# Attention backward pass: dK and dV through column tiles in bursts of four units, crossbar transfers of 1 MB for 512 KB, and TensorE in emission order

## The chip, the cores and the metric

The kernel runs on one core of one Trainium2 chip. The metric is the device time of one execution in microseconds (us), lower is better. Engines: TensorE (PE; its weight loads are PEld), VectorE (DVE), ScalarE (ACT), GpSimd (POOL), and SyncE (SP), whose queue issues the crossbar transfers.

## The reference, cut to what matters

The reference is one transformer block (softmax attention with 32 heads of width 16, sequence 2048, then a squared-ReLU layer) and its gradients for all inputs. Only the attention gradients matter here. For one head, with P the softmax numerators and O the attention output:

```python
scores = einsum('bhqd,bhkd->bhqk', q, k) * scale
p = softmax(scores)
o = einsum('bhqk,bhkd->bhqd', p, v)
# gradients, as the kernel forms them (softmax division and row sums are
# already folded into the operands stored by earlier phases):
#   dS = P * dP          dP = dO V^T
#   dV = P^T dO          dK = dS^T Q          dQ = dS K
```

## The kernel before

The attention backward pass works on *units*: 128 queries, 512 keys, two heads. There are 1024 of them: 8 head groups x 2 head pairs x 4 key chunks x 16 query blocks. dK and dV contract over the queries, which lie on the partitions, so dS and P can be used as they are. dQ contracts over the keys, so dS must be transposed first; a DMA through the crossbar does this. The loop before, cut:

```python
LAG, LAGQ = 2, 3
pup = tile_pool("p5pu", bufs=5); dsp = tile_pool("p5ds", bufs=5); dtp = tile_pool("p5dt", bufs=5)
stp = tile_pool("p5st", bufs=2, space=PSUM); dpp = tile_pool("p5dp", bufs=2, space=PSUM)
...
def kv(u):        # dK, dV of one unit: dS and P are the weights, Q and dO (16 columns) move
    for a in range(2):
        for sub in range(4):
            matmul(acc[:, 0, a, sub, :], lhsT=ds[:, a, sub * P:(sub + 1) * P], rhs=T["Q"][:, ib, col:col + DH], ...)
            matmul(acc[:, 1, a, sub, :], lhsT=pu[:, a, sub * P:(sub + 1) * P], rhs=T["dO"][:, ib, col:col + DH], ...)
    ...
def dq(u):        # dQ of two units: transposed dS is the weights, K (16 columns) moves
    for i in range(2):
        for a in range(2):
            for sub in range(4):
                matmul(accq[:, ib0 + i, a, :], lhsT=dsT[:, (i * 2 + a) * 4 + sub, :], rhs=T["K"][...], ...)
...
for ib0 in range(0, ST, 2):                      # two units
    ds2 = dsp.tile([P, 2, 2, 512], BF16)
    for i in range(2):
        ...                                      # two 512-column matmuls to st, two to dp
        for a in range(2):
            scalar.activation(pu[:, a, :], sts[a][:], Exp, scale=self.scale)
        if len(pend) >= LAG:
            kv(pend.pop(0))
        vector.tensor_tensor(ds2[:, i], dp[:], pu[:], mult)
        pend.append(...)
    dsT = dtp.tile([P, 16, P], BF16)
    sync.dma_start_transpose(dsT[:], ds2[...])   # 512 KB through the crossbar
    if len(pendq) >= LAGQ:
        dq(pendq.pop(0))                         # dQ three transfers behind
    pendq.append(...)
```

The framework's scheduler orders the instructions of each engine.

The softmax here doesn't subtract the row's maximum and nothing guards it: scores larger than these inputs give would overflow.

Of the kernel before, what the change touches and what calls it, by code (L numbers as in the profile page):

```python
# [8 lines left out]
BF16 = mybir.dt.bfloat16  # L9
F32 = mybir.dt.float32  # L10
ACT = mybir.ActivationFunctionType
ALU = mybir.AluOpType
# [6 lines left out]
P = 128  # L19
DH = 16  # L20
# [13 lines left out]
class K:  # L34
# [219 lines left out]
    def phase12(self):  # L254
# [8 lines left out]
        with tc.tile_pool(name="p12", bufs=1) as sb, tc.tile_pool(name="p12e", bufs=8) as eb:  # L263
# [116 lines left out]
            with tc.tile_pool(name="p2c", bufs=1) as cp, tc.tile_pool(name="p2q", bufs=2) as qp, \  # L380
# [12 lines left out]
                for pidx in range(2 * NQ):  # L393
                    g, jp = divmod(pidx, 2)
                    heads = [4 * g + 2 * jp + a for a in range(2)]
                    if jp == 0:
                        T = self.load_quad(qp, srcs, g)
                    KT = T["KT"]
                    self.load_masked(masked, {"QT": (self.QTq_d, 0)}, g, jp)
# [47 lines left out]
                out[n].append(t)  # L447
        return out

    def load_masked(self, masked, srcs, g, jp):  # L450
        nc = self.nc
        for n, (src, sh) in srcs.items():
            for a in range(2):
                j = 2 * jp + a
                r = 32 * ((j + sh) % 4)
                for (c0, cw) in chunks(self.S, 512):
                    nc.sync.dma_start(masked[n][j][r:r + 32, c0:c0 + cw], src[g, r:r + 32, c0:c0 + cw])

    def load_quad(self, pool, srcs, g):
        nc = self.nc  # L460
# [613 lines left out]
    def attn_bwd(self):  # L1074





        tc, nc = self.tc, self.nc  # L1080
        S, D, H, NQ, ST, SC = self.S, self.D, self.H, self.NQ, self.ST, self.SC
        LAG, LAGQ = 2, 3
        W = 4 * DH
        with ExitStack() as es:
            qp = es.enter_context(tc.tile_pool(name="p5q", bufs=2))
            pup = es.enter_context(tc.tile_pool(name="p5pu", bufs=LAG + 3))
            dsp = es.enter_context(tc.tile_pool(name="p5ds", bufs=5))
            dtp = es.enter_context(tc.tile_pool(name="p5dt", bufs=LAGQ + 2))
            stp = es.enter_context(tc.tile_pool(name="p5st", bufs=2, space=PSUM))
            dpp = es.enter_context(tc.tile_pool(name="p5dp", bufs=2, space=PSUM))  # L1090
            accp = es.enter_context(tc.tile_pool(name="p5acc", bufs=1, space=PSUM))
            acckv = accp.tile([P, 2, 2, 2, 4, DH], F32, name="acckv")
            accq = accp.tile([P, ST, 2, DH], F32, name="accq")
            tm = {"K": self.ktm_d, "Q": self.qtm_d, "dO": self.dOp_d}
            fm = {"QT": self.QTq_d, "dOT": self.dOTq_d}
            cp = es.enter_context(tc.tile_pool(name="p5c", bufs=1))
            masked = self.make_masked(cp, ["KT", "VT"])
            pend, pendq = [], []

            def load_group(g):  # L1100
                T = {}
                for n, src in fm.items():
                    t = qp.tile([P, S], BF16, name=f"{n}q")
                    nc.gpsimd.dma_start(t[:], src[g])  # L1104
                    T[n] = t
                for n, src in tm.items():
                    t = qp.tile([P, ST, W], BF16, name=f"{n}g")
                    with nc.allow_non_contiguous_dma(reason="128B runs"):
                        nc.gpsimd.dma_start(t[:], src.rearrange("(st p) d -> p st d", p=P)[:, :, g * W:(g + 1) * W])
                    T[n] = t  # L1110
                return T

            def kv(u):
                (T, g, jp, c, ib, acc, pu, ds) = u
                if ib == 0:
                    nc.vector.memset(acc, 0.0)
                for a in range(2):
                    col = (2 * jp + a) * DH
                    for sub in range(4):
                        nc.tensor.matmul(acc[:, 0, a, sub, :], lhsT=ds[:, a, sub * P:(sub + 1) * P],  # L1120
                                         rhs=T["Q"][:, ib, col:col + DH], start=False, stop=False, skip_group_check=True)
                        nc.tensor.matmul(acc[:, 1, a, sub, :], lhsT=pu[:, a, sub * P:(sub + 1) * P],  # L1122
                                         rhs=T["dO"][:, ib, col:col + DH], start=False, stop=False, skip_group_check=True)
                if ib == ST - 1:
                    h0 = 4 * g + 2 * jp
                    d = self.dk_t[:, 4 * c:4 * c + 4, h0 * DH:(h0 + 2) * DH].rearrange("p s (a d) -> p a s d", a=2)
                    nc.vector.tensor_scalar(d, acc[:, 0], self.scale, None, ALU.mult)
                    d = self.dv_t[:, 4 * c:4 * c + 4, h0 * DH:(h0 + 2) * DH].rearrange("p s (a d) -> p a s d", a=2)
                    nc.vector.tensor_copy(d, acc[:, 1])

            def dq(u):
                (T, g, jp, c, ib0, dsT) = u
                if c == 0 and ib0 == 0:
                    nc.vector.memset(accq[:], 0.0)
                for i in range(2):
                    for a in range(2):
                        col = (2 * jp + a) * DH
                        for sub in range(4):
                            nc.tensor.matmul(accq[:, ib0 + i, a, :], lhsT=dsT[:, (i * 2 + a) * 4 + sub, :],  # L1139
                                             rhs=T["K"][:, 4 * c + sub, col:col + DH], start=False, stop=False,  # L1140
                                             skip_group_check=True)
                if c == SC - 1 and ib0 == ST - 2:
                    h0 = 4 * g + 2 * jp
                    d = self.dq_t[:, :, h0 * DH:(h0 + 2) * DH].rearrange("p s (a d) -> p s a d", a=2)
                    nc.vector.tensor_scalar(d, accq[:], self.scale, None, ALU.mult)

            T = load_group(0)
            n = 0
            for g in range(NQ):
                Tn = load_group(g + 1) if g + 1 < NQ else None  # L1150
                for jp in range(2):
                    self.load_masked(masked, {"KT": (self.KTq_d, 0), "VT": (self.VTq_d, 2)}, g, jp)
                    for c in range(SC):
                        c0 = 512 * c
                        acc = acckv[:, n % 2]
                        n += 1
                        for ib0 in range(0, ST, 2):
                            ds2 = dsp.tile([P, 2, 2, 512], BF16, name="ds")
                            for i in range(2):
                                ib = ib0 + i  # L1160
                                q = slice(ib * P, (ib + 1) * P)
                                sts = [stp.tile([P, 512], F32, name="st") for a in range(2)]
                                dp = dpp.tile([P, 2, 512], F32, name="dp")
                                for a in range(2):
                                    nc.tensor.matmul(sts[a][:], lhsT=T["QT"][:, q], rhs=masked["KT"][2 * jp + a][:, c0:c0 + 512],  # L1165
                                                     start=True, stop=True)
                                for a in range(2):
                                    nc.tensor.matmul(dp[:, a, :], lhsT=T["dOT"][:, q], rhs=masked["VT"][2 * jp + a][:, c0:c0 + 512],  # L1168
                                                     start=True, stop=True)
                                pu = pup.tile([P, 2, 512], BF16, name="pu")  # L1170
                                for a in range(2):
                                    nc.scalar.activation(pu[:, a, :], sts[a][:], ACT.Exp, scale=self.scale)  # L1172
                                if len(pend) >= LAG:
                                    kv(pend.pop(0))
                                nc.vector.tensor_tensor(ds2[:, i], dp[:], pu[:], ALU.mult)  # L1175
                                pend.append((T, g, jp, c, ib, acc, pu, ds2[:, i]))
                            dsT = dtp.tile([P, 16, P], BF16, name="dsT")
                            nc.sync.dma_start_transpose(dsT[:], ds2[:].rearrange("p i a k -> p (i a k)"))
                            if len(pendq) >= LAGQ:
                                dq(pendq.pop(0))  # L1180
                            pendq.append((T, g, jp, c, ib0, dsT))
                T = Tn
            while pend:
                kv(pend.pop(0))
            while pendq:
                dq(pendq.pop(0))

    def phase6(self):
        tc, nc, pp, io = self.tc, self.nc, self.pp, self.io
# [261 lines left out]
```

## Time and profile before

The kernel before takes 3542 us (median of 4 runs, 3530 to 3552). The attention backward pass fills 1646 to 3342 us of the profiled run, 1696 us, about half the span.

The first fence has lines of the profile page's groups of instructions. Columns: line, engine, operation, output and inputs with shapes, count; then busy us and mean ns of one; then the idle time of that engine just before them and what ended most of it.

```profile
L1172 ACT ACTIVATE pu<-st 128x512 bf16<-128x512 f32 x2048 | 1114.5, 594 | 573.7 <-PE st L1165 572.3
L1175 DVE TENSOR_TENSOR ds<-dp,pu 128x1024 bf16<-128x1024 f32 x1024 | 1245.8, 1222 | 391.1 <-ACT pu L1172 251.2
L1165 PE MATMUL st<-KTm,QTq 128*128 128x512 bf16 x2048 | 655.2, 384 | 8.0 <-issue 6.8
L1120 PE MATMUL acckv<-Qg,ds 128*128 128x16 bf16 x8192 | 532.1, 170 | 25.8 <-issue 2.9
L1139 PE MATMUL accq<-Kg,dsT 128*128 128x16 bf16 x8192 | 311.8, 170 | 125.2 <-DMA dsT<-ds 123.1
```

ScalarE waits mostly for TensorE's scores, VectorE for ScalarE, and TensorE seldom waits for anything except the transposed dS. TensorE bounds the pass, by this reading. The next fence, the view of busy time in a stretch, shows the whole pass: TensorE is busy 1543 of 1696 us, at 0.97 of its full clock.

```profile
core 0: us, PE busy (x) PEld busy (x) DVE busy (x) ACT busy (x) POOL busy (x), PEclk, DMA share, GB/s
1646.00:3342.00 1696.00, 1542.76 (x28167) 1016.88 (x28675) 1298.95 (x1251) 1117.68 (x2052) 32.79 (x36) 0.97 1.08 173
```

The timeline of an undisturbed stretch comes next. Columns: start and length in us, engine, line, operation, count, and in brackets the idle time before and what ended it.

```profile
3200.34 5.16 SPq L1178 DMA_TRANSPOSE dsT<-ds  x2
3200.36 0.66 PE L1165 MATMUL st<-KTm,QTq 128*128 128x512 bf16 x2
3200.63 2.49 DVE L1175 TENSOR_TENSOR ds<-dp,pu 128x1024 bf16<-128x1024 f32 x2 [0.32 <-ACT pu L1172]
3200.78 1.08 ACT L1172 ACTIVATE pu<-st 128x512 bf16<-128x512 f32 x2 [0.18 <-PE st L1165]
...
3201.70 0.55 PE L1139 MATMUL accq<-Kg,dsT 128*128 128x16 bf16 x16
3202.10 0.59 PE L1165 MATMUL st<-KTm,QTq 128*128 128x512 bf16 x2
3203.36 0.66 PE L1165 MATMUL st<-KTm,QTq 128*128 128x512 bf16 x2
```

From the scores at 3200.36 to those at 3203.36, two units, pass 3.00 us: 1.50 us a unit. The sixteen dQ matmuls at 3201.70 follow without a wait. The waits view of 1700 to 3300 us (total us, times, longest) shows that such waits exist, but are not the rule:

```profile
ACT pu L1172 <- PE st L1165: 543.7, 929, 9.5
PEld L1139 <- DMA dsT<-ds: 155.9, 97, 9.0
PE accq L1139 <- DMA dsT<-ds: 117.1, 83, 8.1
```

The last two lines see the same stalls twice, once from the weight load and once from the matmul, so they must not be added. More than half of this, and every long one, lies at the start or near a change of the head group, while the next group's loads are in flight as well.

Taking the end of the last ds instruction, the transfer's landing (its last semaphore update) and the start of the first dQ weight load from the trace, a 512 KB transfer lands 6.2 us after ds is ready (median; nine in ten between 4.6 and 9.7), and dQ starts 7.55 us after ds (median). Landed data waits for TensorE for 1.0 us (median), but in 120 of 512 transfers it is TensorE that waits for the landing (dQ starts within 0.1 us of it).

### The profile page before, as it was taken

Reading aid. Unit: us, or ns where it says so; the run is one execution under the profiler, and the core shown is the slowest. Engines: PE = TensorE matmul, PEld = TensorE weight load, DVE = VectorE, ACT = ScalarE, POOL = GpSimd, SP = SyncE. Lnnn points to the kernel's source line nnn. Section 1 sums busy time; section 2 is a strip of 40 time slices with the busy share of each in tenths; the row PEclk is TensorE's granted clock in tenths of the full one; section 3 lists DMA queues with packets and bytes.
Section 4 is the critical chain, followed back from the end, with each engine's and each line's share of the span. In section 5 each row is a group of like instructions: output and inputs, shape, how many; then the busy total and the mean of one; then the engine's idle time right before and its main releaser. Section 6 shows DMA issues by size and latency. Waiting matters only on the chain. (4 is left out here: it accounts for less than half of the span.)

```text
span 3518.2 us, 99351 instructions
## 1 busy us (share of the span) xinstructions
PE 3006.1 (85%) x42822; PEld 1747.5 (50%) x43588; DVE 1908.0 (54%) x2886; ACT 2347.3 (67%) x3545; POOL 251.4 (7%) x343
## 2 busy tenths in 40 slices
PE   5999998888876878487997979989799998999977
PEld 2455543333333333265664656656566665666633
DVE  6222220000004366355886868878687786888855
ACT  3999999999982334333765756756566675767633
POOL 3111110000001014311000000000000000000000
PEclk7999999999997989699998989999899999999998
DMA  3111110000013355655999999999999999999952
GB/s 119 63 50 50 45 38 12 12 6 12 5 49 139 113 196 192 189 154 131 174 179 155 178 162 172 176 174 175 161 175 183 176 178 159 180 178 173 176 185 65
DMA packets 1190469, 449.43 MB, mean 128 GB/s; under 512 B 1097354, under 2 KB 1161484, under 8 KB 1190028
## 3 DMA queue, kind: packets, MB, share of 16 engines
q1 hardware_dynamic: 1159900, 361.61, 57.5%
q0 software_dynamic: 21504, 71.71, 6.9%
q10 hardware_dynamic: 8624, 9.70, 0.8%
q8 instruction: 341, 5.59, 0.6%
q14 instruction: 100, 0.82, 0.1%
HBM read 106.83 MB, written 67.64 MB: 50 GB/s over the span
## 5 line engine op out<-in xcount | busy, mean ns | idle before, releaser
L1172 ACT ACTIVATE pu<-st 128x512 bf16<-128x512 f32 x2048 | 1114.5, 594 | 573.7 <-PE st L1165 572.3
L1175 DVE TENSOR_TENSOR ds<-dp,pu 128x1024 bf16<-128x1024 f32 x1024 | 1245.8, 1222 | 391.1 <-ACT pu L1172 251.2
L412 ACT ACTIVATE pu<-st 128x1024 bf16<-128x1024 f32 x1024 | 940.1, 1376 | 4.7 <-PE accbank L418 4.7
L1165 PE MATMUL st<-KTm,QTq 128*128 128x512 bf16 x2048 | 655.2, 384 | 8.0 <-issue 6.8
L409 PE MATMUL st<-QTm,KTq 128*128 128x512 bf16 x1864 | 566.7, 377 | 6.9 <-ACT pu L412 1.5
L1120 PEld LDWEIGHTS <-ds 128*128 128x128 bf16 x8192 | 502.4, 96 | 119.0 <-issue 8.3
L1120 PE MATMUL acckv<-Qg,ds 128*128 128x16 bf16 x8192 | 532.1, 170 | 25.8 <-issue 2.9
L1122 PE MATMUL acckv<-dOg,pu 128*128 128x16 bf16 x8192 | 528.0, 169 | 0.0
L1122 PEld LDWEIGHTS <-pu 128*128 128x128 bf16 x8192 | 460.4, 96 | 118.3 <-issue 8.4
L418 PEld LDWEIGHTS <-pu 128*128 128x128 bf16 x8192 | 291.2, 96 | 458.7 <-ACT pu L412 408.2
L1168 PE MATMUL dp<-VTm,dOTq 128*128 128x512 bf16 x1539 | 508.7, 385 | 0.5 <-DMA dOTq<-dOTq_d 0.5
L418 PE MATMUL accbank<-Vaug,pu 128*128 128x17 bf16 x8192 | 353.5, 172 | 93.4 <-ACT pu L412 38.1
L1139 PE MATMUL accq<-Kg,dsT 128*128 128x16 bf16 x8192 | 311.8, 170 | 125.2 <-DMA dsT<-ds 123.1
L1139 PEld LDWEIGHTS <-dsT 128*128 128x128 bf16 x8192 | 263.5, 96 | 192.4 <-DMA dsT<-ds 164.6
L1168 PEld LDWEIGHTS <-dOTq 128*128 128x128 bf16 x2048 | 188.4, 97 | 244.7 <-issue 81.3
L427 DVE RECIPROCAL rl<-accbank 128x4 f32<-128x4 f32 x128 | 23.0, 180 | 526.0 <-PE accbank L418 525.6
L288 DVE TENSOR_SCALAR ev_fm<-pps,bcol 128x512 bf16<-128x512 f32 x92 | 69.1, 751 | 195.4 <-PE pps L281 185.7
L409 PEld LDWEIGHTS <-KTq 128*128 128x128 bf16 x2048 | 129.7, 96 | 35.4 <-issue 20.5
L1165 PEld LDWEIGHTS <-QTq 128*128 128x128 bf16 x2048 | 128.9, 96 | 11.1 <-issue 8.1
L281 PE MATMUL pps<-xhat1T,wpad 128*128 128x512 bf16 x372 | 119.9, 378 | 7.8 <-DVE ev_fm L288 3.8
L1104 POOL DMA_DIRECT2D QTq<-QTq_d x8 | 4.5, 558 | 1184.0 <-PE dp L1168 1156.4
L544 ACT ACTIVATE rT<-ups,bias 128x512 bf16<-128x512 f32 x56 | 38.5, 687 | 52.1 <-PE ups L542 52.0
(298 smaller groups left out, 2260.2 us busy)
## 6 DMA issues: line engine op xcount, KB each, us to landing
dsT<-ds SPq DMA_TRANSPOSE x512
rT_d<-rT SPq DMA_DIRECT2D x4, 1792.0 KB
rT<-rT_d SPq DMA_DIRECT2D x4, 1792.0 KB
duT_d<-duT POOLq DMA_DIRECT2D x4, 1792.0 KB, 12.0
rT_f<-rT_d SPq DMA_DIRECT2D x14, 512.0 KB
duT_f<-duT_d POOLq DMA_DIRECT2D x14, 512.0 KB, 4.1
xhat_d<-xhat SPq DMA_DIRECT2D x2, 2048.0 KB
QTq_d<-ev_fm POOLq DMA_DIRECT2D x32, 128.0 KB, 2.1
```

The source lines that it names most:

```text
L281: nc.tensor.matmul(pt[:, :sw], lhsT=wpads[t][:, kt, g, :], rhs=xhat1T[:, kt, s0:s0 + sw], start=(kt == 0), stop=(kt == DT - 1))
L288: nc.vector.tensor_scalar(ev[:, :sw], pt[:, :sw], bc, None, ALU.add)
L409: nc.tensor.matmul(stt[:, a, :qw], lhsT=KT[:, kb * P:(kb + 1) * P], rhs=QTm[a][:, q0:q0 + qw], start=True, stop=True)
L412: nc.scalar.activation(pu[:, :, :qw], stt[:, :, :qw], ACT.Exp, scale=self.scale)
L418: nc.tensor.matmul(acc[:, a, sub, :], lhsT=pu[:, a, sub * P:(sub + 1) * P], rhs=Vaug[:, kb, heads[a], :], start=False, stop=False, skip_gr ...
L1120: nc.tensor.matmul(acc[:, 0, a, sub, :], lhsT=ds[:, a, sub * P:(sub + 1) * P], rhs=T["Q"][:, ib, col:col + DH], start=False, stop=False, s ...
L1122: nc.tensor.matmul(acc[:, 1, a, sub, :], lhsT=pu[:, a, sub * P:(sub + 1) * P], rhs=T["dO"][:, ib, col:col + DH], start=False, stop=False, ...
L1139: nc.tensor.matmul(accq[:, ib0 + i, a, :], lhsT=dsT[:, (i * 2 + a) * 4 + sub, :], rhs=T["K"][:, 4 * c + sub, col:col + DH], start=False, s ...
L1165: nc.tensor.matmul(sts[a][:], lhsT=T["QT"][:, q], rhs=masked["KT"][2 * jp + a][:, c0:c0 + 512], start=True, stop=True)
L1168: nc.tensor.matmul(dp[:, a, :], lhsT=T["dOT"][:, q], rhs=masked["VT"][2 * jp + a][:, c0:c0 + 512], start=True, stop=True)
L1172: nc.scalar.activation(pu[:, a, :], sts[a][:], ACT.Exp, scale=self.scale)
L1175: nc.vector.tensor_tensor(ds2[:, i], dp[:], pu[:], ALU.mult)
```

## The change

The intent is to shorten TensorE's work. With dS and P as the *moving* operand, dK and dV need four 512-column matmuls per unit in place of sixteen pairs of weight load and 16-column matmul. Each of the four has 16 weight columns and occupies one of four column tiles of the array, so that they can run side by side. Because a change of tiling was expected to have a price, the matmuls of four units are done in one burst. The result is now transposed, so 16 TensorE transposes per head pair turn it back ("turn"). The crossbar transfers hold four units (1 MB), TensorE runs in emission order, and the masked K and V loads move to GpSimd's queue, one head pair earlier. The diff, condensed to its core; the turn, the copies of the results, the masked loads and the tail are cut:

```diff
-        LAG, LAGQ = 2, 3
+        G = 4
-            pup bufs=5, dsp bufs=5, dtp bufs=5          (tiles of two units)
+            pup bufs=9, dsp bufs=3, dtp bufs=3          (ds and dsT: four units)
-            acckv = accp.tile([P, 2, 2, 2, 4, DH], F32, name="acckv")
+            acckv = accp.tile([P, 512], F32, name="acckv")
 def kv(u):
+                for j, (n, src) in enumerate((("Q", ds), ("dO", pu))):
+                    for a in range(2):
+                        r = 64 * j + 32 * a
+                        nc.tensor.matmul(acckv[r:r + DH, :], lhsT=T[n][:, ib, col:col + DH], rhs=src[:, a, :],
+                                         start=(ib == 0), stop=(ib == ST - 1))
+            with tc.manual_schedule(engines={mybir.EngineType.PE}):
+                            for ib0 in range(0, ST, G):
+                                dsg = dsp.tile([P, G, 2, 512], BF16, name="ds")
+                                for i in range(G):
+                                    ...                       # scores, [turn], dP, exponentials, product
+                                    pend.append(...)
+                                    if len(pendq) > G:
+                                        dq(pendq.pop(0))      # one unit of dQ
+                                    if i == 1 and len(pend) >= G + 2:
+                                        r = kv_group()        # the burst: four units of kv
+                                dsT = dtp.tile([P, 8 * G, P], BF16, name="dsT")
+                                nc.sync.dma_start_transpose(dsT[:], dsg[:].rearrange("p i a k -> p (i a k)"))
+                                for i in range(G):
+                                    pendq.append((T, g, jp, c, ib0 + i, i, dsT))
```

How far dQ trails the scores is set by the test `len(pendq) > G`: the queue holds eight units when a group begins, so dQ of a unit is emitted eight units after its scores.

More of the change, by code (lines that the diff above doesn't have):

```diff
@@ L448, in make_masked, with load_masked @@
         return out
-    def load_masked(self, masked, srcs, g, jp):
+    def load_masked(self, masked, srcs, g, jp, eng=None):
         nc = self.nc
+        eng = eng or nc.sync
         for n, (src, sh) in srcs.items():
@@ L456, in load_masked @@
                 for (c0, cw) in chunks(self.S, 512):
-                    nc.sync.dma_start(masked[n][j][r:r + 32, c0:c0 + cw], src[g, r:r + 32, c0:c0 + cw])
+                    eng.dma_start(masked[n][j][r:r + 32, c0:c0 + cw], src[g, r:r + 32, c0:c0 + cw])
     def load_quad(self, pool, srcs, g):
@@ L1085, in attn_bwd @@
             qp = es.enter_context(tc.tile_pool(name="p5q", bufs=2))
-            pup = es.enter_context(tc.tile_pool(name="p5pu", bufs=LAG + 3))
-            dsp = es.enter_context(tc.tile_pool(name="p5ds", bufs=5))
-            dtp = es.enter_context(tc.tile_pool(name="p5dt", bufs=LAGQ + 2))
+            pup = es.enter_context(tc.tile_pool(name="p5pu", bufs=9))
+            dsp = es.enter_context(tc.tile_pool(name="p5ds", bufs=3))
+            dtp = es.enter_context(tc.tile_pool(name="p5dt", bufs=3))
+            kvp = es.enter_context(tc.tile_pool(name="p5kv", bufs=2))
             stp = es.enter_context(tc.tile_pool(name="p5st", bufs=2, space=PSUM))
@@ L1091, in attn_bwd @@
             accp = es.enter_context(tc.tile_pool(name="p5acc", bufs=1, space=PSUM))
-            acckv = accp.tile([P, 2, 2, 2, 4, DH], F32, name="acckv")
+            acckv = accp.tile([P, 512], F32, name="acckv")
+            nc.vector.memset(acckv[:], 0.0)
             accq = accp.tile([P, ST, 2, DH], F32, name="accq")
@@ L1096, in attn_bwd @@
             cp = es.enter_context(tc.tile_pool(name="p5c", bufs=1))
+            kvs = cp.tile([P, 1], F32, name="kvs")
+            nc.vector.memset(kvs[0:64], self.scale)
+            nc.vector.memset(kvs[64:P], 1.0)
             masked = self.make_masked(cp, ["KT", "VT"])
@@ L1113, in kv, with turn, dq @@
             def kv(u):
-                (T, g, jp, c, ib, acc, pu, ds) = u
-                if ib == 0:
-                    nc.vector.memset(acc, 0.0)
+                (T, g, jp, c, ib, kvT, pu, ds) = u
+                for j, (n, src) in enumerate((("Q", ds), ("dO", pu))):
+                    for a in range(2):
+                        r = 64 * j + 32 * a
+                        col = (2 * jp + a) * DH
+                        nc.tensor.matmul(acckv[r:r + DH, :], lhsT=T[n][:, ib, col:col + DH], rhs=src[:, a, :],
+                                         start=(ib == 0), stop=(ib == ST - 1))
+                if ib == ST - 1:
+                    nc.vector.tensor_scalar(kvT[:, 512 * c:512 * (c + 1)], acckv[:], kvs[:], None, ALU.mult)
+            def turn(g, jp, kvT):
+                h0 = 4 * g + 2 * jp
+                tp = dpp.tile([P, ST, P], BF16, name="dp")
+                for st in range(ST):
+                    nc.tensor.transpose(tp[:, st, :], kvT[:, st * P:(st + 1) * P], self.ident[:])
+                v = tp[:].rearrange("p s (t a e) -> p t s a e", t=2, a=2)
+                for t, dst in enumerate((self.dk_t, self.dv_t)):
+                    d = dst[:, :, h0 * DH:(h0 + 2) * DH].rearrange("p s (a d) -> p s a d", a=2)
+                    nc.scalar.copy(d, v[:, t, :, :, 0:DH])
+            def dq(u):
+                (T, g, jp, c, ib, i, dsT) = u
+                if c == 0 and ib == 0:
+                    nc.vector.memset(accq[:], 0.0)
                 for a in range(2):
@@ L1119, in kv @@
                     for sub in range(4):
-                        nc.tensor.matmul(acc[:, 0, a, sub, :], lhsT=ds[:, a, sub * P:(sub + 1) * P],
-                                         rhs=T["Q"][:, ib, col:col + DH], start=False, stop=False, skip_group_check=True)
-                        nc.tensor.matmul(acc[:, 1, a, sub, :], lhsT=pu[:, a, sub * P:(sub + 1) * P],
-                                         rhs=T["dO"][:, ib, col:col + DH], start=False, stop=False, skip_group_check=True)
-                if ib == ST - 1:
-                    h0 = 4 * g + 2 * jp
-                    d = self.dk_t[:, 4 * c:4 * c + 4, h0 * DH:(h0 + 2) * DH].rearrange("p s (a d) -> p a s d", a=2)
-                    nc.vector.tensor_scalar(d, acc[:, 0], self.scale, None, ALU.mult)
-                    d = self.dv_t[:, 4 * c:4 * c + 4, h0 * DH:(h0 + 2) * DH].rearrange("p s (a d) -> p a s d", a=2)
-                    nc.vector.tensor_copy(d, acc[:, 1])
-            def dq(u):
-                (T, g, jp, c, ib0, dsT) = u
-                if c == 0 and ib0 == 0:
-                    nc.vector.memset(accq[:], 0.0)
-                for i in range(2):
-                    for a in range(2):
-                        col = (2 * jp + a) * DH
-                        for sub in range(4):
-                            nc.tensor.matmul(accq[:, ib0 + i, a, :], lhsT=dsT[:, (i * 2 + a) * 4 + sub, :],
-                                             rhs=T["K"][:, 4 * c + sub, col:col + DH], start=False, stop=False,
-                                             skip_group_check=True)
-                if c == SC - 1 and ib0 == ST - 2:
+                        nc.tensor.matmul(accq[:, ib, a, :], lhsT=dsT[:, (i * 2 + a) * 4 + sub, :],
+                                         rhs=T["K"][:, 4 * c + sub, col:col + DH], start=False, stop=False,
+                                         skip_group_check=True)
+                if c == SC - 1 and ib == ST - 1:
                     h0 = 4 * g + 2 * jp
@@ L1145, in dq @@
                     nc.vector.tensor_scalar(d, accq[:], self.scale, None, ALU.mult)
-            T = load_group(0)
-            n = 0
-            for g in range(NQ):
-                Tn = load_group(g + 1) if g + 1 < NQ else None
-                for jp in range(2):
-                    self.load_masked(masked, {"KT": (self.KTq_d, 0), "VT": (self.VTq_d, 2)}, g, jp)
-                    for c in range(SC):
-                        c0 = 512 * c
-                        acc = acckv[:, n % 2]
-                        n += 1
-                        for ib0 in range(0, ST, 2):
-                            ds2 = dsp.tile([P, 2, 2, 512], BF16, name="ds")
-                            for i in range(2):
-                                ib = ib0 + i
-                                q = slice(ib * P, (ib + 1) * P)
-                                sts = [stp.tile([P, 512], F32, name="st") for a in range(2)]
-                                dp = dpp.tile([P, 2, 512], F32, name="dp")
-                                for a in range(2):
-                                    nc.tensor.matmul(sts[a][:], lhsT=T["QT"][:, q], rhs=masked["KT"][2 * jp + a][:, c0:c0 + 512],
-                                                     start=True, stop=True)
-                                for a in range(2):
-                                    nc.tensor.matmul(dp[:, a, :], lhsT=T["dOT"][:, q], rhs=masked["VT"][2 * jp + a][:, c0:c0 + 512],
-                                                     start=True, stop=True)
-                                pu = pup.tile([P, 2, 512], BF16, name="pu")
-                                for a in range(2):
-                                    nc.scalar.activation(pu[:, a, :], sts[a][:], ACT.Exp, scale=self.scale)
-                                if len(pend) >= LAG:
-                                    kv(pend.pop(0))
-                                nc.vector.tensor_tensor(ds2[:, i], dp[:], pu[:], ALU.mult)
-                                pend.append((T, g, jp, c, ib, acc, pu, ds2[:, i]))
-                            dsT = dtp.tile([P, 16, P], BF16, name="dsT")
-                            nc.sync.dma_start_transpose(dsT[:], ds2[:].rearrange("p i a k -> p (i a k)"))
-                            if len(pendq) >= LAGQ:
-                                dq(pendq.pop(0))
-                            pendq.append((T, g, jp, c, ib0, dsT))
-                T = Tn
@@ L1183, in attn_bwd, with kv_group @@
-            while pend:
-                kv(pend.pop(0))
-            while pendq:
-                dq(pendq.pop(0))
+            def kv_group():
+                for u in pend[:G]:
+                    kv(u)
+                (T, g, jp, c, ib, kvT, pu, ds) = pend[G - 1]
+                del pend[:G]
+                return (g, jp, kvT) if c == SC - 1 and ib == ST - 1 else None
+            msrc = {"KT": (self.KTq_d, 0), "VT": (self.VTq_d, 2)}
+            self.load_masked(masked, msrc, 0, 0)
+            T = load_group(0)
@@ new lines, in attn_bwd @@
+            turnq = []
+            with tc.manual_schedule(engines={mybir.EngineType.PE}):
+                for g in range(NQ):
+                    Tn = load_group(g + 1) if g + 1 < NQ else None
+                    for jp in range(2):
+                        if 2 * g + jp + 1 < 2 * NQ:
+                            self.load_masked(masked, msrc, (2 * g + jp + 1) // 2, 1 - jp, eng=nc.gpsimd)
+                        kvT = kvp.tile([P, S], BF16, name="kvT")
+                        for c in range(SC):
+                            c0 = 512 * c
+                            for ib0 in range(0, ST, G):
+                                dsg = dsp.tile([P, G, 2, 512], BF16, name="ds")
+                                for i in range(G):
+                                    ib = ib0 + i
+                                    q = slice(ib * P, (ib + 1) * P)
+                                    sts = [stp.tile([P, 512], F32, name="st") for a in range(2)]
+                                    for a in range(2):
+                                        nc.tensor.matmul(sts[a][:], lhsT=T["QT"][:, q], rhs=masked["KT"][2 * jp + a][:, c0:c0 + 512],
+                                                         start=True, stop=True)
+                                    if turnq and i == 3:
+                                        turn(*turnq.pop(0))
+                                    dp = dpp.tile([P, 2, 512], F32, name="dp")
+                                    for a in range(2):
+                                        nc.tensor.matmul(dp[:, a, :], lhsT=T["dOT"][:, q], rhs=masked["VT"][2 * jp + a][:, c0:c0 + 512],
+                                                         start=True, stop=True)
+                                    pu = pup.tile([P, 2, 512], BF16, name="pu")
+                                    for a in range(2):
+                                        nc.scalar.activation(pu[:, a, :], sts[a][:], ACT.Exp, scale=self.scale)
+                                    nc.vector.tensor_tensor(dsg[:, i], dp[:], pu[:], ALU.mult)
+                                    pend.append((T, g, jp, c, ib, kvT, pu, dsg[:, i]))
+                                    if len(pendq) > G:
+                                        dq(pendq.pop(0))
+                                    if i == 1 and len(pend) >= G + 2:
+                                        r = kv_group()
+                                        if r:
+                                            turnq.append(r)
+                                dsT = dtp.tile([P, 8 * G, P], BF16, name="dsT")
+                                nc.sync.dma_start_transpose(dsT[:], dsg[:].rearrange("p i a k -> p (i a k)"))
+                                for i in range(G):
+                                    pendq.append((T, g, jp, c, ib0 + i, i, dsT))
+                    T = Tn
+                turn(*kv_group())
+                while pendq:
+                    dq(pendq.pop(0))
```

## The prediction

It was made from the kernel, the diff and the profile before alone.

> **What bounds it now.** The attention backward pass runs from about 1646 to 3342 us (timeline): 1024 units of four 512-column matmuls, two exponentials, one product, 16 dK/dV ("kv") and 8 dQ weight-load/matmul pairs. In undisturbed stretches (timeline, 3200 to 3235 us) a unit takes 1.50 us, TensorE at full granted clock: wide matmuls 0.85 us, kv 0.41, dQ 0.27. ScalarE needs 1.09 us a unit, VectorE 1.25. 1024 x 1.50 is 1536 us; the other 160 us are mostly seven stalls of about 20 us at the head-group changes (windows near 1860, 2080, 2510 us), where the group's loads compete with the crossbar transfers.
>
> The crossbar is nearly as tight. From the trace's DMA packets and semaphore updates: one 512 KB transfer per 3.0 us; three quarters are issued only after the previous issue ended, then about every 2.9 us. Alone, one lands about 5 us after ds is ready: 1.1 us to the first packet, about 2.45 of packets, over 1 to landing. Undisturbed, dQ starts 7.5 us after ds is ready (timeline), so there are 2.5 us of slack.
>
> **What changes.** kv goes from 0.41 to about 0.21 to 0.28 us a unit: four 512-column matmuls in four column tiles, if they overlap, as the Trainium skill says in TensorEngine Tiling (Array Packing), section Key Properties; it also says that changing the mode drains TensorE, hence the bursts. No run here shows either yet. TensorE's need falls to about 1.35 to 1.40 us a unit; VectorE, about 1.29, is next. About a third of the stage's TensorE instructions go, so fewer instruction fetches interrupt the transfers; masked loads leave SyncE's queue.
>
> **Where it is lost.** A transfer now holds four units: it starts only when the fourth is done and takes about 2.45 us longer, about 7.3 us to landing (estimate: 5 + 2.45). dQ of group n-2 begins in the first unit of group n, on an in-order TensorE: at 1.40 us a unit that leaves only 5 x 1.40 + 0.85 - 2.75 = 5.1 us. The loop over two groups is landing 7.3 + dQ 0.27 + wide 0.85 + dQ 0.27 + burst 1.1 + wide 0.85 + dQ 0.27 + last unit's scores to ds ready 2.75 (timeline) = 13.7 us for eight units: 1.7 us a unit instead of 1.50. Before, this loop has room. With faster packets (1.85 us per 512 KB, seen for short times) it would be 1.55. So TensorE's gain turns into waiting for dsT. At 1.62 to 1.70 us a unit plus about 100 us for group changes and the start the stage takes 1760 to 1840 us.
>
> **Prediction.** 3630 us, 3430 to 3750 us 8 times in 10. Faster by over 2%: 0.22; within 2%: 0.28; slower by over 2%: 0.50.
>
> **What would show it.** Right: the waits view shows TensorE waiting for dsT far above the present 117 us, mostly before the first dQ of each group of four; 1 MB transfers landing 6.5 to 8 us after ds is ready; kv bursts near 1 us. Wrong on tiles: bursts of 3 us or more (no overlap; well slower). Wrong on the loop: dsT waits stay small and units take 1.4 us.
>
> **What would make it wrong.** The larger transfers may stream without the gaps now seen between small ones, or at the fast packet rate with fewer instruction fetches; then VectorE or TensorE bounds the unit at 1.35 to 1.45 us and the kernel gains 3 to 5%. Group-change stalls may shrink with the masked loads a pair earlier.

## The result, and the profile after

The changed kernel takes 3825 us (median of 4 runs, 3815 to 3836), and its results are correct. Ratios here are the mean time of one kernel's fast runs over that of the other's of the same rounds, so not quite the ratio of the quoted medians: 1.080, 95% interval 1.075 to 1.085. The kernel became slower by 8%. The prediction said slower, but by 2.5%, and its range ended at 3750.

The pass now takes 1641 to 3639 us, 1998 us for 1696; nothing else in the program became longer. The groups of instructions after:

```profile
L1194 ACT ACTIVATE pu<-st 128x512 bf16<-128x512 f32 x2048 | 1105.6, 594 | 859.5 <-PE st L1184 857.9
L1184 PE MATMUL st<-KTm,QTq 128*128 128x512 bf16 x2048 | 700.1, 400 | 39.8 <-DMA dOTq<-dOTq_d 7.4
L1149 PE MATMUL accq<-Kg,dsT 128*128 128x16 bf16 x8192 | 362.3, 171 | 366.8 <-DMA dsT<-ds 326.6
L1127 PE MATMUL acckv<-ds,Qg 128*16 128x512 bf16 x2048 | 321.5, 444 | 0.6 <-DVE ds L1195 0.6
```

The idle time before the dQ matmuls went from 125 to 367 us, and ScalarE's wait for scores from 572 to 858 us. The waits of 1700 to 3600 us (the stretch is longer, because the pass is):

```profile
ACT pu L1194 <- PE st L1184: 825.8, 665, 15.0
PEld L1149 <- DMA dsT<-ds: 399.1, 156, 15.0
PE accq L1149 <- DMA dsT<-ds: 310.0, 130, 14.5
```

And the pass as one stretch. The clock that the throttle granted fell from 0.97 to 0.91:

```profile
1641.00:3639.00 1998.00, 1596.32 (x16643) 728.85 (x16642) 1289.77 (x1128) 1124.66 (x2084) 145.72 (x263) 0.91 0.82 147
```

A piece of the timeline shows both what the change gained and where it was lost:

```profile
3400.44 10.91 SPq L1204 DMA_TRANSPOSE dsT<-ds  x2
...
3401.12 0.35 PE L1149 MATMUL accq<-Kg,dsT 128*128 128x16 bf16 x8
3401.40 0.39 PE L1127 MATMUL acckv<-ds,Qg 128*16 128x512 bf16 x2
3401.41 0.39 PE L1127 MATMUL acckv<-pu,dOg 128*16 128x512 bf16 x2
3401.62 0.38 PE L1127 MATMUL acckv<-ds,Qg 128*16 128x512 bf16 x2
...
3402.37 0.60 PE L1184 MATMUL st<-KTm,QTq 128*128 128x512 bf16 x2
...
3404.58 0.35 PE L1149 MATMUL accq<-Kg,dsT 128*128 128x16 bf16 x8
...
3405.21 0.59 PE L1190 MATMUL dp<-VTm,dOTq 128*128 128x512 bf16 x2
...
3408.22 0.36 PE L1149 MATMUL accq<-Kg,dsT 128*128 128x16 bf16 x8 [2.42 <-DMA dsT<-ds]
```

The gain: the first four burst matmuls start within 0.01 us (3401.40 and 3401.41, two each), the next four 0.21 us later. Four matmuls on four column tiles take the time of one, and the burst from 3401.40 to the next scores at 3402.37 takes 0.97 us for four units.

The loss: the transfer issued at 3400.44 is needed by the dQ at 3408.22, 7.78 us later. TensorE was ready for it after the dP matmuls of 3405.21 and stood still for 2.42 us. As TensorE works in order, the scores behind that dQ wait too, and with them ScalarE, VectorE, and the next transfer.

This is a closed loop over two groups of four units: the ds of group n is ready, its transfer lands, its dQ starts while the units of group n + 2 are computed, the ds of group n + 2 is ready, its transfer starts. The terms, read from the trace for every group, with what the prediction had put in. The last column leaves out the 38 of 254 loops that touch a change of the head group, because the prediction counted those changes apart:

```
                                         predicted   measured, mean (median)   away from changes, mean
ds ready -> transfer landed                 7.3        7.7 (7.1) us                 7.3
landed -> first dQ                          0          0.8 (0.04)                   0.8
first dQ -> ds of group n + 2 ready         6.4        7.0 (6.6)                    6.9
sum: two groups, eight units               13.7       15.5                         15.0
```

The mean before rounding is 15.53 us; 128 times that is 1988 us, for a pass of 1998. Before, the same eight units took 4 x 3.30 = 13.2 us on average, stalls included. The short two-group periods of the changed kernel (one in twenty) are 13.0 us (6.73 to dQ, 6.23 after it): the same loop with nothing in its way.

The 0.8 us between landing and dQ can be followed in the trace. In 170 of 256 groups dQ starts within 0.3 us of the landing. The other 86 hold 196 of the 204 us in sum. In all 86 TensorE had stood still before the dQ of the group just before (for 2.8 us, median), in 81 of them until that group's own landing, and after the next landing it was still busy with the work in between, for all but 7 of the 196 us. So the loops of the even and of the odd groups delay each other on the one TensorE that works in order.

### The profile page after: what moved, and what is told of

Read it like the earlier page. It is cut to its first block, busy times and chain, and to the rows that moved or that the text cites. A ratio compares the mean times of both kernels' runs of the same rounds, so it can differ in the third digit from the quotient of the medians.

```text
span 3814.2 us, 75626 instructions
## 1 busy us (share of the span) xinstructions
PE 3094.9 (81%) x31556; PEld 1460.3 (38%) x31556; DVE 1894.1 (50%) x2761; ACT 2354.2 (62%) x3577; POOL 371.1 (10%) x583
## 5 line engine op out<-in xcount | busy, mean ns | idle before, releaser
L1184 PE MATMUL st<-KTm,QTq 128*128 128x512 bf16 x2048 | 700.1, 400 | 39.8 <-DMA dOTq<-dOTq_d 7.4
L1149 PE MATMUL accq<-Kg,dsT 128*128 128x16 bf16 x8192 | 362.3, 171 | 366.8 <-DMA dsT<-ds 326.6
L1190 PE MATMUL dp<-VTm,dOTq 128*128 128x512 bf16 x2048 | 648.4, 400 | 0.3
L1149 PEld LDWEIGHTS <-dsT 128*128 128x128 bf16 x8192 | 351.0, 98 | 676.1 <-DMA dsT<-ds 419.9
L418 PEld LDWEIGHTS <-pu 128*128 128x128 bf16 x8192 | 291.2, 96 | 458.7 <-ACT pu L412 408.2
L1127 PE MATMUL acckv<-ds,Qg 128*16 128x512 bf16 x2048 | 321.5, 444 | 0.6 <-DVE ds L1195 0.6
L1127 PE MATMUL acckv<-pu,dOg 128*16 128x512 bf16 x2048 | 321.5, 444 | 0.0
L458 POOL DMA_DIRECT2D KTm<-KTq_d x120 | 59.8, 503 | 1504.7 <-PE st L1184 1502.7
L1127 PEld LDWEIGHTS <-Qg 128*16 128x16 bf16 x2048 | 80.7, 94 | 90.3 <-issue 41.8
L1127 PEld LDWEIGHTS <-dOg 128*16 128x16 bf16 x2048 | 80.6, 94 | 0.0
```

What stands on the lines that cost most here:

```text
L418: nc.tensor.matmul(acc[:, a, sub, :], lhsT=pu[:, a, sub * P:(sub + 1) * P], rhs=Vaug[:, kb, heads[a], :], start=False, stop=False, skip_gr ...
L458: eng.dma_start(masked[n][j][r:r + 32, c0:c0 + cw], src[g, r:r + 32, c0:c0 + cw])
L1127: nc.tensor.matmul(acckv[r:r + DH, :], lhsT=T[n][:, ib, col:col + DH], rhs=src[:, a, :], start=(ib == 0), stop=(ib == ST - 1))
L1149: nc.tensor.matmul(accq[:, ib, a, :], lhsT=dsT[:, (i * 2 + a) * 4 + sub, :], rhs=T["K"][:, 4 * c + sub, col:col + DH], start=False, stop=F ...
L1184: nc.tensor.matmul(sts[a][:], lhsT=T["QT"][:, q], rhs=masked["KT"][2 * jp + a][:, c0:c0 + 512], start=True, stop=True)
L1190: nc.tensor.matmul(dp[:, a, :], lhsT=T["dOT"][:, q], rhs=masked["VT"][2 * jp + a][:, c0:c0 + 512], start=True, stop=True)
```

## The experiments

Theory A: this loop bounds the changed kernel. dQ trails by eight units, and eight units of work are shorter than the transfer plus the work that must follow it. Rival B: column tiles make TensorE slow, by the switch or by a lower clock. Rival C: the rate of the crossbar is the bound. Rival D: it is the emission order. All diffs are against the changed kernel unless said otherwise. Median of the kernel before: 3539 to 3547 us.

### No wait for the transfer

dQ multiplies a fixed zero tile, so dQ and what follows from it are wrong; the transfers are still made.

```diff
-    matmul(accq[:, ib, a, :], lhsT=dsT[:, (i * 2 + a) * 4 + sub, :], ...)
+    matmul(accq[:, ib, a, :], lhsT=fixT[:], ...)
```

> The changed kernel, but dQ multiplies a fixed zero tile in place of the transposed dS (dQ and what follows from it are wrong on purpose; the transfers are still made, nothing waits for them). Theory A, the loop through the transfer's landing bounds the unit: the wait for dsT goes to zero, the granted clock in the stage returns to about 1.0, the unit falls to 1.41 us (the shortest group of four seen was 5.65 us), the kernel to 3300 to 3400 us. Rival B, column tiles or their low-activity clock make TensorE slow: 3750 to 3830 us, clock still 0.9.

Measured: 3474 us, ratio 0.982 (0.976 to 0.987), clock in the pass 0.96. The loss is gone, with all column tiles and the order in place: against rivals B and D. (This run and the first of the two with the sixteen pairs below were timed twice, all others four times.) But it is not 3300 to 3400: without any wait for dsT a group of four takes 5.85 us (median), not 5.65. The shortest group seen in the changed kernel had been a poor guide. The stalls at the head-group changes are still there too: up to 13 us of waiting for a ds buffer that a transfer had not yet read. Its waits of 1700 to 3250 us have no line of TensorE for dsT any more:

```profile
ACT pu L1196 <- PE st L1186: 498.4, 484, 16.6
DVE ds L1197 <- DMA dsT<-ds: 66.9, 6, 13.3
```

### dQ twelve units behind

```diff
-    dtp = ... bufs=3      pup = ... bufs=9
+    dtp = ... bufs=4      pup = ... bufs=7
-    if len(pendq) > G:
+    if len(pendq) > 2 * G:
```

> The changed kernel with dQ one group later: twelve units behind the scores, not eight; four dsT buffers for three, paid with seven pu buffers for nine. Theory A: the loop is now 7.1 + 6.5 us for twelve units, so it no longer binds; unit 1.41 to 1.5 us, clock about 1.0, kernel 3330 to 3450 us. Rival B (TensorE itself is slower) and rival C (the crossbar's rate binds): stays above 3750 us.

Measured: 3467 us, ratio 0.980 (0.976 to 0.984), clock 0.97, correct. It is near the run without the wait, and just misses its expectation, which had counted on the same short group. The transfers are as large as in the changed kernel and land no sooner (7.5 us, median), so their size is not harmful in itself and their rate not the bound (against rival C).

### Transfers of half the size

```diff
+    if i % 2 == 1:
+        dsT = dtp.tile([P, 16, P], BF16, name="dsT")           # dtp: bufs=6
+        nc.sync.dma_start_transpose(dsT[:], dsg[:, i - 1:i + 1]...)
+        for k in range(2): pendq.append((T, g, jp, c, ib - 1 + k, k, dsT))
-    if len(pendq) > G:
+    if len(pendq) > 6:                                         # still eight units
```

> The changed kernel with two 512 KB transfers per group in place of one of 1 MB, dQ still eight units behind. Theory A: landing 5 to 6 us after ds, and the first half of a group starts two units earlier; the loop has room of about 2 us; the unit is then bounded by the rate of small transfers seen before, about 2.9 us per two units: 1.45 to 1.5 us, kernel 3380 to 3520 us. Rivals B and D (emission order binds): above 3750 us.

Measured: 3442 us, ratio 0.973 (0.969 to 0.976), correct. With eight units of distance kept, half the size removes the loss: the first half of a group leaves two units earlier, and each half lands sooner.

### The scheduler's order

```diff
-    with tc.manual_schedule(engines={mybir.EngineType.PE}):
+    if True:
```

> The changed kernel with TensorE's order left to the scheduler as before. Rival D, the emission order is what costs: 3500 us or less. Theory A: the scheduler may move dQ behind the later scores and so add some lag, but by no more than a unit or two: 3650 to 3850 us.

Measured: 3656 us, ratio 1.033 (1.029 to 1.037), correct. Still slower than before, so the emission order does not explain the loss, though the scheduler takes 169 of the 283 us off. With the scheduler, the way from the first dQ to the next ds is 5.7 us for 7.0 (means, as in the table above), and the clock 0.97. That way is as short, and the time nearly the same, as with nine units of distance below (5.7 us, 3671 us): the scheduler lets dQ slip behind later work, as the expectation had feared. That this is all it does is not shown.

### dQ nine and ten units behind: the dose

One constant, no buffers:

```diff
-    if len(pendq) > G:
+    if len(pendq) > G + 1:     # nine units
+    if len(pendq) > G + 2:     # ten units (the other run)
```

> The changed kernel with dQ nine units behind the scores, not eight; no buffer changes. Theory A: the loop of two groups loses one unit's work of about 1.12 us between landing and the next issue: 7.1 to 7.7 (landing) + about 5.2 = 12.3 to 12.9 us, above the 11.7 us that TensorE and ScalarE need; still bound, but less: 3530 to 3630 us, between the changed kernel and the twelve-unit one. A theory in which eight units were just short of some fixed threshold, or in which the seven pu buffers of the twelve-unit run made the gain: no such step in between.

> The changed kernel with dQ ten units behind; a change of one constant, still three dsT buffers and nine pu buffers. Theory A: 7.1 to 7.7 + about 3.1 = 10.2 to 10.8 us, under 11.7: the loop no longer binds; 3455 to 3490 us, like the twelve-unit run. If the buffers made that run's gain: above 3600 us.

Measured: nine units 3671 us, ratio 1.038 (1.034 to 1.042); ten units 3450 us, ratio 0.975 (0.971 to 0.979). The steps eight, nine, ten, twelve give 3825, 3671, 3450 and 3467 us: the time falls with each unit of distance until the loop has room, then no further. The expectation for nine ended 40 us too low, for the same reason as the prediction: 5.3 us after dQ starts holds for the groups at full clock, but the mean was 5.7, the landing took 7.9 on average, 0.8 us lay between the two, and so the mean period was 14.3 us. The one for ten was missed by 5 us, on the fast side. The pass with ten units and its waits (1700 to 3250 us):

```profile
1644.00:3265.00 1621.00, 1460.04 (x16367) 713.03 (x16636) 1273.53 (x1128) 1121.79 (x2084) 145.81 (x262) 0.98 1.03 181
```

```profile
ACT pu L1194 <- PE st L1184: 465.5, 531, 11.8
PEld L1149 <- DMA dsT<-ds: 93.3, 54, 11.9
PE accq L1149 <- DMA dsT<-ds: 77.1, 35, 11.4
```

The pass is 377 us shorter than in the changed kernel by one constant; the clock is back at 0.98, and the wait for dsT below what it was before the change. The timeline of this run shows what holds the unit up once the loop does not:

```profile
2703.80 0.39 PE L1127 MATMUL acckv<-ds,Qg 128*16 128x512 bf16 x2
...
2704.77 0.60 PE L1184 MATMUL st<-KTm,QTq 128*128 128x512 bf16 x2
2705.19 2.15 ACT L1194 ACTIVATE pu<-st 128x512 bf16<-128x512 f32 x4 [1.31 <-PE st L1184]
...
2710.62 0.61 PE L1184 MATMUL st<-KTm,QTq 128*128 128x512 bf16 x2
2711.05 1.08 ACT L1194 ACTIVATE pu<-st 128x512 bf16<-128x512 f32 x2 [1.31 <-PE st L1184]
```

From 2704.77 to 2710.62 it is 5.85 us for four units, 1.46 a unit. After each burst ScalarE has stood idle for 1.31 us. There are two st buffers, one unit's worth, so ScalarE has no scores to work on while TensorE is in the burst, and TensorE then has to wait for ScalarE to free them: in the trace both st matmuls of the next unit start 0.05 us after an exponential ends. This is read from the trace; no run with more st buffers tested it. So the whole gain of the change in a steady unit is 1.50 to 1.46.

### The sixteen pairs of before in place of the column tiles

Twice: in the changed kernel, and in the version with transfers of half the size.

```diff
-    four matmuls into acckv[r:r + DH, :], then turn()
+    the sixteen matmuls of the kernel before into acckv[:, c % 2], copied out by VectorE
```

> The changed kernel (1 MB, eight units, emission order, bursts) but with dK and dV from the sixteen weight-load and matmul pairs of before, no column tiles. Theory A: still bound by the loop, with a burst of about 1.65 us for 1.05: two groups take about 0.5 us more than the changed kernel's: 3830 to 3920 us. Rival B, column tiles make the loss: 3560 us or less.

> The version with two 512 KB transfers per group, but with the sixteen pairs of before for dK and dV. Theory A: the loop has room, so here the column tiles are worth their TensorE time: the burst is longer by 1.65 - 1.05 us, less what the mode switch costs: about 6.3 to 6.5 us a group for 5.85, 3540 to 3600 us. If the tiles are worth nothing: 3440 us.

Measured: 3925 us, ratio 1.109 (1.103 to 1.115), in the changed kernel; 3576 us, ratio 1.011 (1.006 to 1.015), with the half-size transfers (6.40 us a group). Both correct; the first is 5 us above what was expected. The column tiles are innocent of the loss (rival B falls), and are worth 134 us where the loop has room (3576 to 3442), the work of turning the result included. The other parts of the change, without the tiles and with the loop mended, are slightly slower than the kernel before.

### More work for TensorE just before the wait

The halved clock needed a test of its own: is it only a sign of the waits, or does it cost time? The first dP matmuls of each group are done three times over, with the same result.

```diff
+    for r in range(2 if i == 0 else 0):
+        for a in range(2):
+            nc.tensor.matmul(dp[:, a, :], lhsT=T["dOT"][:, q], rhs=masked["VT"][2 * jp + a][:, c0:c0 + 512], start=True, stop=True)
```

> The changed kernel with its first pair of dP matmuls in each group of four done three times over (same values, same place): 0.85 us more TensorE work a group, just before the wait for dsT, where TensorE mostly stands idle. In the changed kernel's profile the way from the first dQ to the next ds takes 6.46 us at full granted clock and 8.1 to 9.5 us in the groups where the clock was halved. If the halved clock is itself a cost of the waits: more work keeps the clock up, and the kernel gets faster, 3700 to 3800 us, clock in the stage above 0.94. If the clock is only a sign of the waits and costs nothing: the same 3825 us, or more by up to 100 us where TensorE came late anyway.

Measured: 3765 us, ratio 1.063 (1.060 to 1.066), against 1.080 for the changed kernel, correct. More work made the kernel 1.6% faster (1.063 against 1.080). The pass with the extra matmuls:

```profile
1649.00:3588.00 1939.00, 1705.69 (x17658) 810.40 (x17659) 1293.11 (x1128) 1125.36 (x2084) 145.35 (x263) 0.97 0.84 151
```

TensorE is busy for 109 us more and the pass is 59 us shorter, at a clock of 0.97 for 0.91. The trace has 363 us at half clock in the changed kernel's pass, and 113 us here. The way from the first dQ to the next ds fell from 7.0 to 6.6 us; in the groups at full clock it stayed at 6.4 to 6.5. So the clock costs time, and it makes the loop worse: the half clock goes with the waits, and the half-speed matmuls lie on the loop. The expectation's 9.5 us, though, is mostly not the clock's: see the head-pair changes below.

### Both, scheduler order with half size, and the loop in the kernel before

Half-size transfers with dQ twelve units behind (threshold 10, eight dsT buffers, seven pu buffers); half-size transfers with the scheduler's order; and the kernel *before* with `LAGQ = 2` for 3, which also takes one of its five dsT buffers, as their number is `LAGQ + 2`.

> Two 512 KB transfers per group, dQ twelve units behind, eight dsT buffers of half size, seven pu buffers. Steady units cannot get shorter (5.85 us a group with and without a bound loop), so all that is left to gain are the stalls at the seven group changes, about 13 us each with eight units: 3400 to 3440 us if the added lag bridges them, 3440 us if the ds buffers hold it up as well.

> Two 512 KB transfers per group with TensorE's order left to the scheduler. If emission order is needed for the bursts: the scheduler breaks them up or moves them, 3480 to 3560 us. If it does not matter: 3440 us.

> The kernel of before with dQ two transfers behind, not three. Theory A applied to it: the loop is then three transfers of two units, 9.0 us at its pace, for a landing of 5 to 6.2 us and about 4.5 us of work after it, 9.5 to 10.7: bound, 3600 to 3800 us. If the loop is a matter of the changed kernel's order alone: 3540 us.

Measured, all correct: 3413 us, ratio 0.964 (0.961 to 0.967); 3422 us, ratio 0.966 (0.964 to 0.968); and 3623 us, ratio 1.022 (1.020 to 1.025). The last shows that the loop is a matter of distance in the old kernel as well: one transfer less of distance costs 2.2%, and TensorE's weight loads wait for dsT 154 times in place of 97 (1700 to 3300 us). For the second, the branch "emission order is needed" (3480 to 3560 us) was wrong, and it was 18 us faster than the other branch's 3440: the scheduler's order does no harm, so emission order is not needed for the bursts once the loop has room. The first is the best version, about 130 us faster than the kernel before and 410 us faster than the changed one; between it and the second the intervals overlap. In its steady stretches a group still takes 5.86 us; the extra distance gains at the head-group changes (groups of over 8 us exceed the median by 63 us in sum, for 94 us with eight units). Of these 63 us, 51 are another stall, which distance does not touch: once after each change of the head pair dQ waits for VectorE to empty and clear accq, of which there is one. Both the changed kernel (first line, 1700 to 3600 us) and this one (second line, 1700 to 3250 us) have it:

```profile
PE accq L1149 <- DVE accq L1145: 39.6, 14, 2.8
PE accq L1149 <- DVE accq L1145: 41.6, 15, 3.0
```

No run tried a second accq.

## Why the prediction was right or wrong

- **The bound before, 1.50 us a unit with TensorE first, the transfers close behind:** right, as far as tested. A distance of two transfers in place of three makes the old kernel 2.2% slower. "Before, this loop has room" was generous: 1.0 us (median) between landing and dQ, and none in 120 of 512.
- **The column tiles overlap, burst near 1.1 us:** right. Four start within 0.01 us, the next four 0.21 us later; a burst with its switches takes about 1.05 us at full clock. Without them the mended version loses 134 us.
- **TensorE's need falls to 1.35 to 1.40 us a unit:** too low. Where the loop has room a unit takes 1.46, it seems because during the burst ScalarE has no scores (1.31 us idle after each) and TensorE then waits for the st buffers. This did not decide the result, but it limits what the change can gain as it stands.
- **A 1 MB transfer lands about 7.3 us after ds, too late for eight units of distance:** right, 7.1 us median. The waits for dsT grew from 156 to 399 us in the weight loads' line. Ten units of distance, or half the size, remove the loss.
- **The sum, 13.7 us for eight units:** this is the step that failed, in size; the path was right. It measured 15.0 us away from the head-group changes and 15.5 with them. The prediction added the terms at full clock and with no other delay, and read a steady period from it. Away from the changes the landing measured 7.3 us, as predicted. What was missing is 0.8 us between landing and dQ, which the sum did not have (the two loops delay each other on TensorE, as shown above), and about 0.5 us of the work after it: 6.9 for 6.4 us. Over all groups that work measured 7.0: 6.5 us in the 180 groups at full clock, 8.1 in the 58 at 0.6 to 0.8 of it. The extra-work run shows that the clock costs time. Of the 16 groups between 0.8 and 1 (9.5 us), 12 follow a head-pair change, where dQ waits up to 2.8 us for accq as well, so they do not measure the clock alone; without the groups at head-pair changes the mean is 6.8. On top of the sum, the prediction took 1.62 to 1.70 us a unit, which is less than the 1.71 of its own 13.7 us. 1.3 us x 128 is 166 us; the centre of the prediction was 195 us too low.
- **What stays open:** how the 0.8 us and the slower clock share the loss. The one follows from the trace and the other from the extra-work run, but waits and half clock come together, and no run has the one without the other.
- **"About 100 us for group changes":** fair. 15.5 for 15.0 us is an estimated 70 us over 128 loops.

The odds were 0.50 for slower by over 2%, so the direction was called but hardly with confidence; the range was too narrow on the slow side, because it had room for a loop with fast packets but none for a loop that slows itself.

## What to carry to other kernels

When a transfer is made larger, keep in mind what waits for it: count the units of work between the transfer's start and its first use, and compare their time with the time to the landing and the work that must follow it, not with the transfer rate. Where an in-order engine waits for it inside a loop, sum the loop once around, and add to it: here two such loops shared one engine and delayed each other, and the repeated waits went with a lower clock (0.91 for 0.97), in which the work on the loop takes longer. Distance is often the cheapest remedy: here one constant was worth 375 us, while the faster matmuls that were the point of the change were worth 134.

## What the Trainium skill lacked or had wrong

- *TensorEngine Tiling (Array Packing)*, Key Properties, says that tiles operate independently and that a mode switch drains TensorE, with no cost for the switch. Here four column tiles do run side by side (four 512-column matmuls per 0.21 us), and a burst of sixteen with both switches takes about 1.05 us, some 0.2 us above the 0.86 us of its matmuls. Its section PSUM Bottleneck warns of evacuation; what shows here once the loop has room is the reverse, the engine behind TensorE starved during the burst (1.31 us idle).
- *DMA: Bandwidth & Descriptors*, in its rules for kernel authors, gives "Max bandwidth" as at least 1 MiB per DMA. In a loop with a fixed distance the 1 MB transfers made the kernel 8% slower, and 512 KB at the same distance 2.7% faster than before. The same rules say to issue a DMA early and to wait for it late; the page does not say how to find out how early is enough.
- The same page, under Latency and other measured facts, gives a transpose bandwidth of 261 GB/s where the middle dimension is not contiguous and 350 to 400 where it is. In its anatomy of a DMA it gives about 2.0 us of fixed cost for the GpSimd path; that page has no fixed cost for a transpose. Here the packets of a 512 KB transpose took 2.66 us (median, kernel before) and those of 1 MB 5.05 (changed kernel): 2.4 us per further 512 KB, an estimated 220 GB/s. In the changed kernel 1.18 us lay between issue and first packet and 0.52 between last packet and landing (medians), an estimated 1.7 us that does not depend on the size.
- *TensorE: Matmul & The Clock Gate*, HAM oscillation, states the rule "no PE-idle gaps >~3.4µs" and shows the case of waits of 3 to 5 us. The mechanism agrees with this trace (half clock in pieces of 3.41 us, 363 us of it in the pass), but shorter waits, repeated, went with it too: of 73 such pieces or runs of pieces, 53 had no idle gap above 3.4 us in the 7.5 us before them, and the median of the longest gap was 2.8 us. A later section of the page names frequent micro-idles as a second way, without a length. Beyond the advice there to pad a thin M, the page does not say that filler work can pay; here 0.85 us of it per group of about 7.5 us made the kernel 1.6% faster.
